# Starting the first Strassen quad of the z2 stage among the banded tiles of the last attention group

## Chip, cores, metric

One core of a Trainium2 chip. The metric is the device time of one execution in microseconds (us). Each time below is a median, with the lowest and highest run where they matter.

## The reference

```python
x = A_x                                         # 2048 tokens, 1024 wide
g = sigmoid((x * gate_w).sum(-1, keepdims=True))
# a: 32 heads of 32; each token sees 8 tokens at distances 0, 2, .. 14
logits = einsum('bhsd,bhswd->bhsw', q, kg) * Dh ** -0.5
a = einsum('bhsw,bhswd->bhsd', softmax(masked(logits)), vg) ... @ wo
# b: gMLP mixer
z  = gelu(x @ w_in)                             # 3584 wide: z1 and z2, 1792 each
gg = w_sp @ layernorm(z2) + b_sp
b  = (z1 * gg) @ w_out
return g * a + (1 - g) * b
```

## The kernel before

Matrix products run on the tensor engine (PE), the large ones as Strassen-Winograd "quads": seven products for four tiles, chained through banks of the accumulator memory (PSUM). The logits of the window attention are computed as "bands": small matmuls (L355) whose bank is evicted by ScalarE (ACT, L363), stored to memory, and loaded back in attention layout. Softmax and the products with v run elementwise on VectorE (DVE). There are eight groups of four heads. While PE multiplies for z2 and then for z1, DVE works off the rest of the attention.

One quad; `yield` separates its products:

```python
def chain(..., vs, put, share, N, flip=False, side=None, lean=False, done=None):
    def plus(out, a):
        dve(N / 960.0 + 0.14, clock["PE"] + 0.2)             # the program's own model
        last_add[0] = nc.vector.tensor_tensor(out[:, n], a[:, n], vs, ALU.add)   # L474
    if side is None:
        side = quad[0] % 2                                   # which four banks
        quad[0] += 1
    X, Y, Z, V = bank_roles[side]
    ...
    product(X, pairs(A11, B11), True, N)
    last_seed[0] = nc.scalar.copy(Y[:, n], X[:, n])          # L487, the seed
    yield
    product(V, pairs(S1, T1), True, N)
    share(vs, V[:, n])                                       # L493 on ACT; on DVE in later z1 quads
    yield
    product(Y, pairs(S2, T2), False, N)
    plus(Z, Y)
    yield
    product(X, pairs(A12, B21), False, N)
    put(0, 0, X)                                             # gelu on ACT
    yield
    product(Y, pairs(S3, T3), False, N)
    plus(V, Y)
    ...
    product(Z, pairs(S4, B22), False, N)                     # needs the first add
    ...
```

Four terms recur. The seed is the copy of X into Y (L487). The share copy, or vs copy, is the copy of V into vs (L493). The adds (L474) add vs to other banks. A mark (L559) is a short matmul that PE runs on a bank before products add onto a copied seed there.

The order of DVE's instructions is fixed when the kernel is built. The program keeps a clock for each engine. Before every add or copy it calls `advance`, which places attention operations that its model says still fit:

```python
FR, LATE, WZ_LATE = 0.4, 0.5, 4.0
def advance(t):
    while True:
        events  = [(max(i[0], clock["SP"]), 0, i) for i in due]              # DMA issues
        events += [(sub_end[g] + LATE, 1, g) for g in range(NG)              # exponentials
                   if sub_end[g] < FAR and not hold[0]]
        events += [(max(o[0], clock["DVE"]) + FR * o[1], 2 + n, o)           # DVE operations
                   for n, o in enumerate(options())]
        events = [v for v in events if v[0] <= t]
        if not events: break
        ... # emit the earliest
```

So an operation of length d is put ahead of an add that is due at t if its start plus 0.4 d is not after t. The attention products of one group half:

```python
for ws in SPLIT[g > FINE]:                # FINE = -1: always 4 operations of 2048 elements, L677
    yield ..., lambda: tt(p5[:, ws], in0[:, ws], in1[:, ws], ALU.mult)
for n, ws in enumerate([slice(0, 4)] if g <= FINE else [slice(0, 2), slice(2, 4)]):
    yield ..., lambda: tt(a, a, b, ALU.add)                    # L681, two operations
yield ...                                                      # L682, L686
```

The places that the change touches:

```python
BAND_AT = (1, 3, 6)
def among_bands(g, quad):
    for n in range(7):
        next(quad); step()
        if n + 1 in BAND_AT: band_set(g, x); ...
...
# group_tiles(7):
    return [tiles[0], band[1], tiles[1], band[0], tiles[2], band[2], tiles[3]]
...
for n in range(0, len(quads), 2):         # z2: 15 quads, two at a time
    def quad_step():
        hold[0] = count[0] != 1           # exponential held since group 7: at step 1
        if n == 0 and count[0] == 0: mark(bank_roles[1][1:3], ZC)
        step()
        count[0] += 1
    run(*[z2_quad(*q) for q in quads[n:n + 2]], step=quad_step)
```

The z1 loop:

```python
DRAIN, SUMS = 1, NFH - 2
for fp in range(NFH):
    run(z1_quad(fp, 0), z1_quad(fp, 1), ...)     # DVE makes the share copies from fp = 2 on
    if fp == DRAIN:
        drain()        # place all attention work that is left, here, as one block
```

## Time and profile before

| | before |
|---|---|
| time, median of 3 (lowest to highest) | 650.38 us (650.0 to 650.91) |
| span of the profiled run | 649.2 us |
| PE busy | 638.1 us, 98% |
| DVE busy | 519.3 us, 80% |

PE, busy for 98% of the span, sets the time here. A wait of PE is seen in the timeline as a number in brackets after its line, with the instruction that released it. What another engine costs in this kernel is read from such waits, so the reading goes from PE's waits to the engine named and then back along that engine's order. The prediction shows the lines.

### The profile page before, as it was taken

The numbers are of one execution on the slowest core, as the hardware profiler recorded it, in microseconds if no ns is written. First come the engines' busy times: TensorE is split into PE (matmuls) and PEld (weight loads), VectorE is DVE, ScalarE is ACT, GpSimd is POOL, SyncE is SP. The second block draws the span as 40 slices with busy tenths as digits, with TensorE's granted clock in tenths as the row PEclk, the third lists the DMA queues.
The fourth block names the chain that finished last, engine by engine and source line by source line (L and its number), as shares of the span: only waits on it lengthen the run. The fifth ranks groups of instructions, "written<-read, shape, count | busy, mean of one in ns | idle before, by whom it ended". The sixth has DMA issues, their size and how long they took to land.

```text
span 649.2 us, 11298 instructions
## 1 busy us (share of the span) xinstructions
PE 638.1 (98%) x4346; PEld 336.4 (52%) x4391; DVE 519.3 (80%) x816; ACT 297.8 (46%) x644; POOL 15.4 (2%) x27
## 2 busy tenths in 40 slices
PE   8999999999999999999999999999999999999997
PEld 4544467444445555444444444444444444868684
DVE  0357988999899999999988766987569999596952
ACT  3547677676776877799643121121121121212110
POOL 2210000000000000001000000000000000000000
PEclk9999999999999999999999999999999999999999
DMA  9979564798688012258994578469587383665401
GB/s 207 198 179 269 126 152 103 175 230 200 122 214 204 1 42 85 66 148 230 258 269 133 130 163 172 120 195 280 100 189 172 86 157 99 111 138 128 124 27 49
DMA packets 227174, 98.19 MB, mean 151 GB/s; under 512 B 174496, under 2 KB 214064, under 8 KB 227120
## 3 DMA queue, kind: packets, MB, share of 16 engines
q1 hardware_dynamic: 226256, 95.70, 61.2%
q0 software_dynamic: 576, 1.57, 0.9%
q8 instruction: 34, 0.56, 0.3%
q10 hardware_dynamic: 288, 0.20, 0.1%
q14 instruction: 20, 0.16, 0.1%
HBM read 44.31 MB, written 36.61 MB: 125 GB/s over the span
## 4 chain that ended last, share of the span: by engine, by line
PE 84%; ACT 4%; DVE 4%; DMA 4%; SPq 2%; issue 2%; ACTq 0%; DVEq 0%
PE psum_all L403 69%; PE psum_all L1487 8%; PE psum_all L293 4%; PE psum_all L303 2%; DMA band_d<-arena 2%; ACT arena L839 2%; PE psum_all L355 1%; DVE arena L677 1%; ACT arena L1178 1%; SPq L189 1%; DVE arena L681 1%; SPq L178 1%; DMA arena<-in_A_wqkv_dram 1%; SPq L194 1%; DVE psum_all L474 1%
## 5 line engine op out<-in xcount | busy, mean ns | idle before, releaser
L403 PE MATMUL psum_all<-arena 128*128 128x512 f16 (+6 forms) x2482 | 503.0, 362 | 3.4 <-issue 0.6
L403 PEld LDWEIGHTS <-arena 128*128 128x128 f16 (+1 forms) x2518 | 245.1, 98 | 253.8 <-issue 4.0
L677 DVE TENSOR_TENSOR arena<-arena,att_A 128x2048 f16<-128x2048 bf16 x64 | 75.5, 1219 | 0.3
L474 DVE TENSOR_TENSOR psum_all<-psum_all,arena 128x512 f32<-128x512 f32 (+1 forms) x78 | 51.0, 669 | 10.1 <-PE psum_all L403 8.3
L1487 PE MATMUL psum_all<-arena 128*128 128x256 f16 (+1 forms) x468 | 51.6, 273 | 0.0
L1487 PEld LDWEIGHTS <-arena 128*128 128x128 f16 x468 | 45.8, 98 | 5.5
L293 PE MATMUL psum_all<-arena 128*128 128x512 bf16 x183 | 42.0, 379 | 1.4 <-issue 0.8
L421 ACT COPY psum_all<-psum_all 128x512 f32<-128x512 f32 (+1 forms) x24 | 12.5, 521 | 66.8 <-PE psum_all L403 66.2
L784 ACT ACTIVATE arena<-psum_all 128x448 bf16<-128x448 f32 x64 | 34.3, 546 | 19.0 <-PE psum_all L403 9.0
L1178 ACT ACTIVATE arena<-psum_all 128x512 bf16<-128x512 f32 x56 | 31.4, 612 | 19.8 <-PE psum_all L403 9.0
L681 DVE TENSOR_TENSOR arena<-arena 128x2048 f16<-128x2048 f16 x32 | 37.9, 1218 | 0.0
L363 ACT CAST arena<-psum_all 128x1988 f16<-128x1988 f32 (+3 forms) x25 | 34.0, 1360 | 3.6 <-PE psum_all L355 3.4
L839 ACT ACTIVATE arena<-arena 128x896 bf16<-128x896 bf16 x32 | 30.9, 980 | 0.0
L546 DVE TENSOR_TENSOR arena<-arena 128x512 f16<-128x512 bf16 (+5 forms) x60 | 30.1, 534 | 0.3
L445 ACT COPY psum_all<-psum_all 128x512 f32<-128x512 f32 (+1 forms) x24 | 12.4, 519 | 37.2 <-PE psum_all L403 36.6
L293 PEld LDWEIGHTS <-arena 128*128 128x128 bf16 x192 | 18.1, 98 | 21.6 <-DMA arena<-in_A_wqkv_dram 0.7
L870 ACT CAST arena<-psum_all 128x512 bf16<-128x512 f32 x40 | 22.1, 592 | 12.5 <-DVE psum_all L474 9.6
L389 DVE TENSOR_TENSOR arena<-arena 128x2048 f16<-128x2048 bf16 x8 | 9.4, 1222 | 21.8 <-ACT gl_s L306 20.9
L427 ACT COPY arena<-psum_all 128x512 f32<-128x512 f32 (+1 forms) x24 | 12.7, 534 | 26.3 <-PE psum_all L403 22.5
L487 ACT COPY psum_all<-psum_all 128x512 f32<-128x512 f32 (+1 forms) x39 | 21.7, 570 | 6.6 <-PE psum_all L403 6.0
L432 ACT COPY psum_all<-psum_all 128x512 f32<-128x512 f32 (+1 forms) x24 | 12.5, 519 | 25.6 <-PE psum_all L403 23.0
L550 DVE TENSOR_TENSOR arena<-arena 128x1024 f16<-128x1024 f16 (+1 forms) x16 | 11.3, 714 | 15.7 <-PE psum_all L403 15.7
(113 smaller groups left out, 530.6 us busy)
## 6 DMA issues: line engine op xcount, KB each, us to landing
arena<-v_d SPq DMA_DIRECT2D x8, 960.0 KB, 7.1
z_d<-arena SPq DMA_DIRECT2D x14, 512.0 KB, 3.4
arena<-z_d SPq DMA_DIRECT2D x14, 512.0 KB, 4.1
zg_d<-arena SPq DMA_DIRECT2D x56, 128.0 KB, 2.2
arena<-zg_d SPq DMA_DIRECT2D x32, 224.0 KB, 3.2
band_d<-arena SPq DMA_DIRECT2D x28, 248.5 KB, 4.6
arena<-in_A_wqkv_dram SPq DMA_DIRECT2D x16, 256.0 KB, 4.3
o_d<-arena SPq DMA_DIRECT2D x4, 1024.0 KB, 6.3
```

Source lines behind the costliest of these rows:

```text
L293: nc.tensor.matmul(ps[:], w[:, t, kt, :], xT[:, kt, 512 * c:512 * (c + 1)], start=(kt == 0), stop=(kt == KT - 1))
L363: nc.scalar.copy(dst, src)
L403: nc.tensor.matmul(bank[:, 0:N], lhsT, rhs, start=(start and m == 0), stop=(m == n - 1), skip_group_check=True)
L474: last_add[0] = nc.vector.tensor_tensor(out[:, n], a[:, n], vs, ALU.add)
L546: return [lambda a=a: nc.vector.tensor_tensor(*a) for a in args]
L677: lambda ws=ws, in0=in0, in1=in1: tt(p5[:, ws], in0[:, ws], in1[:, ws], ALU.mult)), False
L681: lambda a=p3[:, ws], b=p3[:, ws.start + 4:ws.stop + 4]: tt(a, a, b, ALU.add)), not n
L784: nc.scalar.activation(z2[:, i + 8 * a, ZC * c:ZC * (c + 1)], bank[:, 0:ZC], ACT.Gelu_apprx_tanh, accum_out=s1[:, 4 * n + c:4 * n + c + 1])
L839: return nc.scalar.activation(junk, src, ACT.Square, accum_out=(s2, s2h)[x][:, n:n + 1])
L870: nc.scalar.copy((qT_slots, kT_slots)[t][g % 2][:, :, 256 * (c + 2 * x):256 * (c + 2 * x + 1)], bank[:].rearrange("p (n e) -> p e n", e=2))
L1178: last_gelu[0] = nc.scalar.activation(z1s[:, f, a, :], bank[:], ACT.Gelu_apprx_tanh)
L1487: nc.tensor.matmul(bank[:, h], l, r, start=(start and m == 0), stop=(m == len(ab) - 1), skip_group_check=True)
```

## The change

Intent: fill PE's wait among the last bands with the first product of the first z2 quad; evict the third band set of group 2 sooner; let the share copies of the first pair go before the exponential that is held back while group 7 is placed; and save DVE time by wider attention operations, placed while PE works on groups 5 to 7. No arithmetic is added or removed.

Counting in the traces, groups from 0: the exponential held is the seventh of eight, that of group 6. The core of the diff:

```diff
-                for ws in SPLIT[g > FINE]:
+                for ws in SPLIT[not wide[0]]:
...
-                for n, ws in enumerate([slice(0, 4)] if g <= FINE else [slice(0, 2), slice(2, 4)]):
+                for n, ws in enumerate([slice(0, 4)] if wide[0] else [slice(0, 2), slice(2, 4)]):
...
-            if n + 1 in BAND_AT:
+            if n + 1 in (BAND_AT if g != 2 else (1, 3, 5)):
...
-            tiles = [lambda a=a, m=m: z2_tile(7, a, m) for m in range(2) for a in range(2)]
+            roles = bank_roles[0]
+            tiles = [lambda n=n: z2_tile(7, n % 2, n // 2, lambda: roles[3 - n % 2]) for n in range(4)]
...
-        return [tiles[0], band[1], tiles[1], band[0], tiles[2], band[2], tiles[3]]
+        early.append(z2_quad(*quads[0], 0))
+        return [tiles[0], band[1], tiles[1], lambda: next(early[0]), band[0], tiles[2], band[2], tiles[3]]
...
         hold[0] = g == NG - 1
+        wide[0] = g in (5, 6, 7)
...
+    wide[0] = False
...
         def quad_step():
-            hold[0] = count[0] != 1
-            if n == 0 and count[0] == 0:
-                mark(bank_roles[1][1:3], ZC)
+            hold[0] = count[0] != 4
             step()
...
-        run(*[z2_quad(*q) for q in quads[n:n + 2]], step=quad_step)
+        two = [z2_quad(*q, m) for m, q in enumerate(quads[n:n + 2])]
+        if n == 0:
+            two = [two[1], early[0]]
+            next(early[0])
+            quad_step()
+            mark(bank_roles[1][1:3], ZC)
+        run(*two, step=quad_step)
```

Since each z2 quad now names its side, the shared counter that gives z1 quads their sides no longer moves by 15 in the z2 stage.

More of the change, by code (lines that the diff above doesn't have):

```diff
@@ L692, in products @@
             next_v()
+    wide = [False]
     SPLIT, FINE = [[slice(n * x, n * x + n) for x in range(8 // n)] for n in (4, 2)], FINE_TO
@@ L785, in z2_gelu, with z2_tile @@
                              accum_out=s1[:, 4 * n + c:4 * n + c + 1])
-    def z2_tile(i, a, m):
-        ps = low_bank()
+    def z2_tile(i, a, m, bank=low_bank):
+        ps = bank()
         pe(2 * T_Z)
@@ L912, in play_group @@
         return True
+    early = []
     def group_tiles(g):
```

## The prediction

> **What bounds the kernel now.** I read the head of the page first, then the longest waits of the tensor engine, then the chain of waits, then the timeline of the 20 us that the change touches.
>
> The page, parts 1 and 2:
>
> ```profile
> span 649.2 us, 11298 instructions
> PE 638.1 (98%) x4346; PEld 336.4 (52%) x4391; DVE 519.3 (80%) x816; ACT 297.8 (46%) x644; POOL 15.4 (2%) x27
> PE   8999999999999999999999999999999999999997
> PEclk9999999999999999999999999999999999999999
> ```
>
> The tensor engine (PE) is busy for 638 of 649 us at full clock. A change that removes no matmul can therefore win at most the 11 us of idle time[...]. The change removes none: it moves four matmuls of one product and leaves the marks (the two short matmuls per bank pair) as many as they were.
>
> Busy time of the engines in stretches of the timeline (columns: stretch and length, then busy us and instruction count of PE, PEld, DVE, ACT, POOL, then clock and DMA):
>
> ```profile
> 80.00:89.00 9.00, 8.40 (x105) 4.93 (x103) 8.37 (x17) 7.71 (x15) 0.00 (x0) 1.00 0.54 125
> 174.00:183.00 9.00, 8.38 (x165) 4.46 (x163) 8.72 (x15) 7.80 (x12) 0.00 (x0) 1.00 0.48 91
> 183.00:194.00 11.00, 10.59 (x56) 5.27 (x54) 10.97 (x15) 8.08 (x19) 0.00 (x0) 1.00 0.85 236
> 194.00:232.00 38.00, 38.00 (x202) 19.66 (x201) 36.84 (x51) 28.33 (x79) 0.00 (x0) 1.00 0.37 93
> ```
>
> The rest of the z2 stage (194 to 232) has no PE idle time at all. What the change can reach is the 0.6 us of each of the first two stretches and 0.4 us of the third. The fourth row also gives the price of a z2 product: 38.00 us over 202 matmuls is 0.188 us each, so 0.75 us for four. DVE, at 10.97 of 11 us, is full just where the first z2 quads run.
>
> The timeline of group 7 and the first quads (start, length, engine, line, count, idle before it and who ended it):
>
> ```profile
> 175.08 1.28 ACT L784 ACT_TABLE_LOAD   x1
> 176.91 1.81 ACT L363 CAST arena<-psum_all 128x1988 f16<-128x1988 f32 x1
> 178.77 0.27 PE L355 MATMUL psum_all<-arena 32*64 32x64 bf16 x16 [0.62 <-ACT arena L363]
> ...
> 184.01 4.62 DVE L677 TENSOR_TENSOR arena<-arena,att_A 128x2048 f16<-128x2048 bf16 x4
> 185.38 1.28 ACT L631 ACT_TABLE_LOAD   x1
> 186.67 0.63 ACT L631 ACTIVATE att_L<-att_L 128x512 f16<-128x512 f16 x1
> 187.21 0.95 ACT L493 COPY arena<-psum_all 128x448 f32<-128x448 f32 x2
> 188.88 1.16 DVE L474 TENSOR_TENSOR psum_all<-psum_all,arena 128x448 f32<-128x448 f32 x2
> 189.56 10.68 PE L403 MATMUL psum_all<-arena 128*128 128x448 f16 x54 [0.27 <-DVE psum_all L474]
> ```
>
> Two waits are seen. (1) The 16-matmul band set waits 0.62 us until ScalarE (ACT) has evicted the band set before it. (2) The fifth product of the first quad waits for the add L474. Two things hold that add: its operand, the copy L493, stands behind the exponential and its table load (until 187.7 and 188.2), and DVE itself is in four attention products until 188.63. Both end within half a microsecond of each other, so removing one alone gains little.
>
> The chain of waits says where the lateness of DVE comes from:
>
> ```profile
> 170.23 3.55 DMA band_d<-arena
> 173.82 2.09 DVE arena L546 x2
> ...
> 184.09 4.55 DVE arena L677 x4
> 188.70 0.09 issue
> 188.81 0.07 issue
> 188.88 1.16 DVE psum_all L474 x2
> 190.03 2.26 DVE arena L681 x2
> 192.29 0.56 DVE psum_all L474
> 192.89 59.22 PE psum_all L403 x312
> ```
>
> From 173.8 to 192.9 the path that sets the end runs through DVE, not ACT, and it began at a band transfer; DVE had stood 2.88 us waiting for the band loads just before 169.4.
>
> [...] the trace has 1219 ns for L677. [...] 1024 elements (L686) take 0.69 us and 2048 take 1.22, so 0.53 us per 1024 and the rest fixed. [...] The load is 1283 ns here, but the exponential starts at 186.67, 1.29 us after the load began[...]; I count 1.28. [...]
>
> **The change, part by part.**
>
> Third band set of group 2 one product earlier. Before, the mark waits for its eviction (end 85.13) with an idle gap of 0.35 us. Evicted some 0.4 us sooner, that gap closes. But at 88.03 PE waits again, for a seed copy behind a vs copy that ACT could start only at 87.23, when the second band set's store landed (87.13) and its buffer was free. That store starts at 81.45 either way. So PE arrives 0.35 us earlier at the same wall: gain about 0.
>
> First product among the bands. It puts 0.75 us of work in front of the set that waited; the start of that set was 969 ns after the matmul before it, where about 300 is usual at such a switch, so 0.66 us of wait is filled. Its seed copy (0.52 us on ACT) delays the next eviction, which then ends about 180.7, as PE arrives (180.6): minus 0.1. Gain 0.55 us. The first z2 section product now starts at 182.70 + 0.75 - 0.66 = 182.8.
>
> Exponential at step 4 instead of step 1. Both vs copies now precede the 3.2 us block of two table loads and the exponential: the adds' operands are there at 184.3 and 186.9 instead of 187.7 and 188.2. Eight gelus follow the block at about 0.52 us each (rate of a dense run), until 194.7; the next pair's third products need their seeds at about 196. No new wait on ACT.
>
> Wide operations in groups 5 to 7. Four L677 in 4.62 us become two of 1.22 + 2 x 0.53 = 2.28, with the usual 0.09 overlap 4.47 us; two L681 in 2.35 become one of 2.28. With three or four half groups touched this is 0.5 us of DVE; most of it lies before the 169.4 wait for the bands, which swallows it. About 0.13 us is left when the products of (group 5, first half) start: 183.9.
>
> The sum at the fifth product. The early quad needs its first add sooner: the fifth product follows the second by six products and two marks, 182.8 + 6 x 0.75 + 0.37 = 187.7, where the old one was ready at 182.7 + 8 x 0.75 + 0.37 = 189.1. DVE does not come sooner: by the program's own placement rule (an operation goes in front of an add if 0.4 of it fits before the add is due) both wide products are still put before the add. They end at 183.9 + 4.47 = 188.4, then 0.2 for the weights (L661) and 0.6 for the add: 189.2. So PE waits about 1.6 us there, against 0.43 before. The second wait (0.31 us at 192.9) goes, since the later adds are then far ahead of their products.
>
> Sum: -0.55 (bands) - 0.31 (second wait) + 1.2 (first wait longer) = +0.3 us. Checked by the other route: the pair ends seven products after 189.3, at 194.5; before, 192.89 + 2 x 0.75 = 194.4. Near nothing; the DVE chain sets both.
>
> **Rivals.** (a) The author's hope: the exponential was what held the adds, DVE is on time, and the waits go. For it: vs arrived at 187.7 to 188.2. Against it: DVE busy until 188.63, chain through DVE. It gives -0.66 - 0.43 - 0.31 = -1.4, and with 0.3 of the group 2 gap 648.7. (b) Coarse operations: a 2.28 us operation put before an urgent add costs up to 1.1 us more than a 1.22 us one, and delays repeat at later pairs: +1 to +2, 651.5 to 652. Against it: wide operations end with group 7, and from 194 to 260 the trace shows PE without a wait over 0.1 us, so slack exists. (c) The exponential later starves attention: its weights start only at 201.06 and 233.1, 14 us after each exponential, so 3 us do no harm: 0. (d) The z2 quads no longer take turns by the shared counter, so the first z1 quad follows the last z2 quad on the same four banks; the gelus there ended at 263.8 to 264.9 and its second product starts near 266: 0 to 0.2.
>
> **Range and chances.** My working gives 650.4 + 0.3; I give rival (a), whole or half, 40%, which pulls to 650.2. Eight in ten: 648.9 to 651.2. A gain of 2% would be 13 us, more than all idle time: 0.4%. A loss of 13 us would need a stall in every quad: 1%.
>
> **What would show it.** Right: the 16-matmul band set starts without its 0.62 us wait; the fifth product of the early quad is released by L474 with an idle time over 0.8 us while its vs copy ended before 185; the seed wait near 88 grows to about 0.6. Wrong: no wait on L474 near 188 (then rival a), or waits on L474 in later pairs (b), or on L487 at the second pair, where I see none.

The sum is -0.55 - 0.31 + 1.2 = +0.3 us, on 650.4, and with its 40% for rival (a) 650.2. The 0.53 us per 1024 elements is measured: L686 (1024 elements) takes 0.69 us, L677 (2048) 1.22, L1146 (4096) 2.29. Why a mark has to precede a product that adds onto a seed is not shown by any run; that the mark moves with the product is in the diff.

## The result

| | before | changed |
|---|---|---|
| median of six runs | 650.45 us | 650.96 us |
| lowest to highest | 650.0 to 651.83 | 650.68 to 654.17 |

A ratio here and below is from the runs of both kernels in the same rounds. It lies near the ratio of the means, and is not quite that of the medians. Here it is 1.0013, with a 95% interval of 0.9992 to 1.0034: the same, within 2%. The profiled run of the changed kernel was its longest, 654.17 us at a mean granted clock of 0.997; the other five took 650.68 to 651.48 at 1.0.

Page of the changed kernel:

```profile
span 652.4 us, 11330 instructions
PE 643.1 (99%) x4391; PEld 336.9 (52%) x4391; DVE 519.6 (80%) x807; ACT 298.4 (46%) x644; POOL 15.9 (2%) x27
PEclk9999999999989999999999999999999999999999
```

Line numbers of this kernel are shifted further down: L784 became L785, and L1174 became L1185. DVE has 9 instructions fewer, but is no less busy. PE has the same 4391 weight loads as before (45 matmul records are missing from the trace of before, so the two busy times compare only roughly; the 11 us of idle time that the prediction counts are too many for the same reason: the changed kernel, with all 4391 records, is idle for 9.3 us, though it has new waits of 2.38 and 0.91 us). New is one digit of its clock, an 8, in the slice around 190 us.

Stretches of the same run (stretch and length, then busy us and count of PE, PEld, DVE, ACT, POOL, then granted clock and DMA):

```profile
80.00:89.00 9.00, 8.71 (x107) 5.36 (x106) 8.62 (x17) 8.17 (x15) 0.00 (x0) 1.00 0.56 128
174.00:183.00 9.00, 9.00 (x168) 4.72 (x167) 8.79 (x11) 8.51 (x14) 0.00 (x0) 1.00 0.62 124
190.16:193.15 2.99, 2.99 (x10) 1.21 (x8) 2.99 (x4) 1.29 (x4) 0.00 (x0) 0.50 0.97 304
194.00:197.00 3.00, 3.00 (x18) 1.56 (x16) 2.15 (x3) 2.15 (x8) 0.00 (x0) 1.00 1.10 301
```

The first two rows are the stretches whose idle time the change was after: PE's idle time there fell from 0.60 to 0.29 and from 0.62 to 0. The third row is new: for 3 us the granted clock was 0.50, and 10 matmuls ran where 18 run in as long a stretch just after it.

Timeline of group 7 and the first quads, changed kernel:

```profile
170.36 0.29 DVE L640 TENSOR_TENSOR att_m<-att_L 128x256 f16<-128x256 f16 x1 [3.94 <-DMA att_L<-band_d]
...
178.52 0.27 PE L355 MATMUL psum_all<-arena 32*64 32x64 bf16 x16
...
183.41 0.53 ACT L493 COPY arena<-psum_all 128x448 f32<-128x448 f32 x1
184.83 4.48 DVE L677 TENSOR_TENSOR arena<-arena,att_A 128x4096 f16<-128x4096 bf16 x2
...
189.23 0.62 DVE L474 TENSOR_TENSOR psum_all<-psum_all,arena 128x448 f32<-128x448 f32 x1
189.91 25.30 PE L403 MATMUL psum_all<-arena 128*128 128x448 f16 x124 [2.38 <-DVE psum_all L474]
```

The band set at 178.52 no longer waits. The share copy is done before 184. The two wide attention operations stand ahead of the add, as predicted, but they start at 184.83, and PE waits 2.38 us instead of 0.27. The first line shows where that began: DVE waited 3.94 us for the loaded bands (2.88 before). L640 computes the maxima of a group's logits; these are the sixth of eight, so the bands are those of group 5. Where expectations below speak of the bands or the maxima of group 7, they mean this wait.

The place that the prediction never looked at is 100 us later, between the second and the third pair of z1 quads. DVE before:

```profile
285.87 3.48 DVE L677 TENSOR_TENSOR arena<-arena,att_A 128x2048 f16<-128x2048 bf16 x3
289.28 2.35 DVE L681 TENSOR_TENSOR arena<-arena 128x2048 f16<-128x2048 f16 x2
...
293.53 1.28 DVE L1174 COPY arena<-psum_all 128x512 f32<-128x512 f32 x2
```

And DVE in the changed kernel, with PE's line after it:

```profile
288.42 4.62 DVE L677 TENSOR_TENSOR arena<-arena,att_A 128x2048 f16<-128x2048 bf16 x4
292.96 2.36 DVE L681 TENSOR_TENSOR arena<-arena 128x2048 f16<-128x2048 f16 x2
...
297.21 1.28 DVE L1185 COPY arena<-psum_all 128x512 f32<-128x512 f32 x2
...
299.16 2.10 PE L403 MATMUL psum_all<-arena 128*128 128x512 f16 x9 [0.91 <-DVE psum_all L474]
```

This is the block that `drain` places ahead of the share copies of the third pair: 3 + 2 + 1 (L682) + 1 (L686) = 7 operations before, 7.74 us; 4 + 2 + 1 + 1 = 8 in the changed kernel, 8.88 us. The share copies and the adds behind them come one operation later, and PE, which had no wait there, stands idle for 0.91 us; the stage becomes 1.05 us longer.

For the experiments I cut each trace at PE's own landmarks: the marks (L559) ahead of the v quads, of group 3, of the z2 quads and of the z1 quads, the first z2 tile, and the first matmul of the last stage. Lengths in us:

| stage | before | changed, profiled run | difference |
|---|---|---|---|
| first mark to v-quad mark (holds group 2's bands) | 20.11 | 19.81 | -0.30 |
| to the mark at group 3 | 39.62 | 39.51 | -0.11 |
| to the first z2 tile | 49.48 | 49.49 | 0 |
| z2 tiles to z2 mark, without the early product (0.75) | 9.17 | 8.49 | -0.68 |
| z2 quads, with the same product (0.75) taken off before's | 79.86 | 83.42 | +3.56 |
| z1 quads and mixing by w_sp, to the last stage | 283.94 | 284.99 | +1.05 |
| sum, first mark to last stage | 486.45 | 489.98 | +3.53 |

Each sum also holds the early product (0.75) and 3.51 us between the two pairs of z1 marks, which are in no row.

The z2 row holds a wait (2.38 us) and the half-rate stretch: from 190.16 to 193.15 matmuls start 373 ns apart instead of 189, nine of them, which is 1.7 us.

### The profile page after: what moved, and what is told of

Read it like the earlier page. It is cut to its first block, busy times and chain, and to the rows that moved or that the text cites. A ratio compares the mean times of both kernels' runs of the same rounds, so it can differ in the third digit from the quotient of the medians. Undisturbed runs are those within 1.5% of the kernel's fastest.

```text
span 652.4 us, 11330 instructions
## 1 busy us (share of the span) xinstructions
PE 643.1 (99%) x4391; PEld 336.9 (52%) x4391; DVE 519.6 (80%) x807; ACT 298.4 (46%) x644; POOL 15.9 (2%) x27
## 4 chain that ended last, share of the span: by engine, by line
PE 86%; DVE 5%; ACT 4%; DMA 2%; issue 2%; SPq 1%; DVEq 0%
PE psum_all L403 70%; PE psum_all L1498 8%; PE psum_all L293 5%; PE psum_all L303 2%; ACT arena L840 2%; DVE arena L677 2%; PE psum_all L355 1%; ACT arena L1189 1%; DMA band_d<-arena 1%; DVE psum_all L474 1%; DVE arena L681 1%; SPq L178 1%; DVE arena L546 1%; DMA arena<-in_A_wqkv_dram 1%; DMA att_L<-band_d 0%
## 5 line engine op out<-in xcount | busy, mean ns | idle before, releaser
L677 DVE TENSOR_TENSOR arena<-arena,att_A 128x2048 f16<-128x2048 bf16 (+1 forms) x58 | 75.0, 1329 | 0.2
L474 DVE TENSOR_TENSOR psum_all<-psum_all,arena 128x512 f32<-128x512 f32 (+1 forms) x78 | 51.5, 671 | 13.5 <-PE psum_all L403 11.4
L785 ACT ACTIVATE arena<-psum_all 128x448 bf16<-128x448 f32 x64 | 34.3, 544 | 18.6 <-PE psum_all L403 9.6
L681 DVE TENSOR_TENSOR arena<-arena 128x2048 f16<-128x2048 f16 (+1 forms) x29 | 37.6, 1328 | 0.0
L546 DVE TENSOR_TENSOR arena<-arena 128x512 f16<-128x512 bf16 (+5 forms) x60 | 30.1, 535 | 0.4
L487 ACT COPY psum_all<-psum_all 128x512 f32<-128x512 f32 (+1 forms) x39 | 21.7, 568 | 7.3 <-PE psum_all L403 6.6
L303 PE MATMUL psum_all<-arena 128*128 128x385 bf16 x128 | 22.5, 329 | 0.5 <-DVE arena L325 0.3
```

The costliest lines, as they stand in the source:

```text
L303: nc.tensor.matmul(ps[:, 0:VP + 1], xT[:, kt, i * P:(i + 1) * P], wvp[:, kt, :], start=(kt == 0), stop=(kt == KT - 1))
L546: return [lambda a=a: nc.vector.tensor_tensor(*a) for a in args]
L677: lambda ws=ws, in0=in0, in1=in1: tt(p5[:, ws], in0[:, ws], in1[:, ws], ALU.mult)), False
L681: lambda a=p3[:, ws], b=p3[:, ws.start + 4:ws.stop + 4]: tt(a, a, b, ALU.add)), not n
L785: nc.scalar.activation(z2[:, i + 8 * a, ZC * c:ZC * (c + 1)], bank[:, 0:ZC], ACT.Gelu_apprx_tanh, accum_out=s1[:, 4 * n + c:4 * n + c + 1])
```

## The experiments

**Theory**, as it stood after all runs (the fourth term came out of experiment 4). Four terms: group 2 gains up to 0.4; the filled band wait gains 0.68; the first add loses time that depends on when the bands land; and the early start shifts DVE's placement so that one more attention product falls into the drain, +1.06. **Rivals:** the wide operations cause the losses, as coarser steps (the prediction's rival b); the later exponential causes them (its rival c); the changed sides of the banks cause them (its rival d); or the profiled run was an accident and nothing was lost.

Twelve runs were made, on three chips in three sets, all correct. "x / y" is the median of a kernel and of the kernel before in the same rounds. All differ from the kernel before by under 2%.

**1. No early product.** The changed kernel, with the first product back behind the bands:

```diff
-        return [tiles[0], band[1], tiles[1], lambda: next(early[0]), band[0], tiles[2], band[2], tiles[3]]
+        return [tiles[0], band[1], tiles[1], band[0], tiles[2], band[2], tiles[3]]
```

> The changed kernel, but the first z2 quad begins after group 7 again (the exponential stays late, the operations wide, the group 2 band early). Theory A (the early start makes the first add due about 1.4 us sooner than DVE can give it): the wait for L474 at the fifth product falls from 2.4 us to 1.0 to 1.3, the 0.62 us wait of the 16-matmul band set comes back, and the time is 0.3 to 0.7 us under the changed kernel's. Rival B (the wide operations alone make the wait): the wait stays over 2 us and the time is 0.5 us above the changed kernel's.

651.2 / 651.25, ratio 0.9996 (0.9979 to 1.0014). The band wait is back, by its old releaser:

```profile
180.11 0.27 PE L355 MATMUL psum_all<-arena 32*64 32x64 bf16 x16 [0.61 <-ACT arena L363]
```

Waits on L474 at the first pair are 0.10 and 0.15 us, less than the expected 1.0 to 1.3, the z1 stage is 283.93, and the drain has 7 operations. So the long first wait and the longer z1 stage both need the early start; wide operations and the late exponential, which this kernel keeps, make neither by themselves. First mark to last stage is 485.85, 0.60 less than before.

**2. Only the third band set of group 2.** The kernel before with

```diff
-            if n + 1 in BAND_AT:
+            if n + 1 in (BAND_AT if g != 2 else (1, 3, 5)):
```

> The kernel before with nothing but the third band set of group 2 one product earlier. The comparison of the two traces says that this part alone gains 0.40 us (the marks' wait of 0.35 us is gone and the seed wait near 88 is not longer). My prediction said 0, with a seed wait near 88 grown to 0.6 us. Expected: 0.4 us under before, PE starts the fourth row of the v quads near 87.6 in place of 88.0.

652.29 (650.47 to 656.6) / 651.25, ratio 1.0024 (0.9996 to 1.0052). The time shows no gain. The trace does: the first two stages are 19.82 and 39.51, 0.29 and 0.11 shorter than before, and the whole stretch to the last stage is 485.79, 0.66 shorter. Its runs scatter over 6 us, one at a clock of 0.997; a gain of 0.4 us cannot be read from them. Of the 0.66, 0.26 lies in z2, where the maxima came 0.26 us sooner than before. For the edit itself, all traces help: the first two stages together take 59.73 and 59.76 in the two without it (before and experiment 9), and 59.32 to 59.60 in the twelve with it. So the part gains 0.13 to 0.41, and the prediction's "about 0" was too low.

**3. Weight sums placed sooner.** The changed kernel with the sums of z2 weights (L546) released to DVE earlier in the model, so that fewer stand ahead of the first add:

```diff
-    FR, LATE, WZ_LATE = 0.4, 0.5, 4.0
+    FR, LATE, WZ_LATE = 0.4, 0.5, 1.5
```

> The changed kernel with the four sums of the z2 weights (L546, 1.05 us each) placed 2.5 us sooner in the order, into the time in which DVE stands waiting for the bands of group 7 (3.9 us in the changed kernel). Theory A (DVE is late at the first add because of that idle time): DVE idle before the maxima falls under 2 us, the add comes about 2 us sooner, the wait at the fifth product falls from 2.4 us to under 0.7, and the time is 1.5 to 2 us under the changed kernel's. Rival C (the first add is held by ACT, its copy of vs or the exponential): the wait stays over 1.5 us.

651.0 / 651.25, ratio 1.0 (0.9982 to 1.0019). The first wait fell to 0.23 us, and the z2 stage to 79.58; the z1 stage stayed at 285.00, with 8 operations in the drain and the same wait:

```profile
295.40 6.85 PE L403 MATMUL psum_all<-arena 128*128 128x512 f16 x31 [0.91 <-DVE psum_all L474]
```

So the z1 loss is a term of its own, and not a consequence of PE's long wait in z2. The times do not show the 1.5 to 2 us that were expected (651.0 beside the changed kernel's 650.96, from other rounds).

**4. DVE's model clock set forward as well.** Experiment 3 with

```diff
         hold[0] = g == NG - 1
+        if g == NG - 1:
+            clock["DVE"] += 2.0
```

so that adds go ahead of attention work in z2.

> As the run with the sums sooner, and the program's own clock for DVE is set 2.0 us later at the start of group 7, so that it puts fewer attention operations in front of the first add (two narrow ones in place of two wide ones). Theory A: no wait over 0.3 us for L474 in the first pair, and none over 0.5 us near 298; the time is 649.0 to 649.6 us, about 1 us under before. Rival C: the wait stays. Rival D (work pushed behind the add comes back as a wait in the z1 stage): the wait near 298 grows over 1.5 us.

655.9 (655.28 to 657.34) / 651.25, ratio 1.0072 (1.0053 to 1.009). This is not the gain that the edit was made for; the expectation's rival D came true. The z2 stage is the shortest of all, 78.91, with no wait at the first pair. But the attention work put off was not gone: the drain holds 11 operations, 12.12 us, and the z1 stage took 291.23:

```profile
298.43 4.00 PE L403 MATMUL psum_all<-arena 128*128 128x512 f16 x9 [4.37 <-DVE psum_all L474]
```

After these 4.37 us the clock was 0.50 for about 5 us, with matmuls 427 ns apart instead of 216; all six runs had a mean clock of 0.995 to 0.997. This was the run that showed me the drain as the place to look: 7 operations no wait, 8 a wait of 0.91, 11 a wait of 4.37. Three operations more are 3.24 us of DVE and 3.46 us of wait.

**5. The changed kernel again.** No edit.

> The changed kernel once more, for a profile in which the tensor engine keeps its full clock. Theory A: the same waits as in the first profile, 2.4 us at the fifth product of the early quad and 0.9 us near 298, and where no stretch of half-rate matmuls follows, the part from the group 1 marks to the last stage takes about 488.1 us, 1.7 us over before. If the half rate follows every such wait, it takes 490 us again.

651.68 (650.44 to 653.4) / 651.66, ratio 0.9996 (0.9974 to 1.0018). In this profiled run DVE waited 2.85 us for the bands, PE waited

```profile
189.10 7.16 PE L403 MATMUL psum_all<-arena 128*128 128x448 f16 x37 [0.94 <-DVE psum_all L474]
```

and no stretch at half rate followed. The z1 stage was 285.00 again. So the 2.38 us and the half rate belong to single executions, and the 1.06 to the kernel. First mark to last stage is 486.93; the expected 488.1 took the wait of 2.4 us for granted.

**6. Narrow operations.** The changed kernel without

```diff
-        wide[0] = g in (5, 6, 7)
```

> The changed kernel with the narrow attention operations in groups 5 to 7. Then three narrow products stand before the first add in place of two wide ones (3.5 us in place of 4.5). Theory A with the width as part of it: the wait at the fifth product falls from 2.4 us to 0.7 to 1.4; the wait near 298 stays at 0.9 us, since the attention work left for the drain is the same. Rival E (width has no part in it): it stays at 2.4 us.

651.44 / 651.66, ratio 0.9997 (0.9978 to 1.0016). The expectation was a wait of 0.7 to 1.4 us at the fifth product; the fifth product now finds its add done: the add starts 18.01 us after the maxima (L640) instead of 18.87. The wait moved to a later product:

```profile
192.79 67.74 PE L403 MATMUL psum_all<-arena 128*128 128x448 bf16 x356 [0.63 <-DVE psum_all L474]
```

The z1 stage is 284.99, the drain has 8 operations. The width moves the first add by 0.86 us; it has no part in the z1 loss.

**7. DVE's model clock set back in z2, and experiment 3.**

```diff
+        if n == 4:
+            clock["DVE"] -= 0.6
         count = [0]
```

The model then takes DVE for free 0.6 us sooner, and by the second z1 pair it has placed one attention product more ahead of the drain.

> The changed kernel with the z2 weight sums sooner (as in the third run) and the program's clock of DVE set back 0.6 us at the third pair of z2 quads, so that one or two more attention operations are placed before the drain. Theory F (each attention operation left for the drain after the second z1 quad pair is paid by PE): seven or fewer operations stand between the last add of that pair and the first DVE copy in place of eight, the wait of 0.9 us near 298 is gone, and the part from the group 1 marks to the last stage takes 485.0 to 485.2 us, 1.3 us under before. Rival G (the new taking of turns by the banks causes the wait near 298): it stays at 0.9 us.

649.29 (649.15 to 650.66) / 651.66, ratio 0.9964 (0.9946 to 0.9983): the fastest kernel, 0.36% under the kernel before, with an interval that excludes 1 (experiment 10 is the only other faster one of which that holds). The drain is back to three L677, and PE then runs from the first z1 products to the end of the mixing by w_sp without a break that the view shows, 216 ns for each matmul:

```profile
265.89 284.04 PE L403 MATMUL psum_all<-arena 128*128 128x512 f16 x1314
284.12 3.49 DVE L677 TENSOR_TENSOR arena<-arena,att_A 128x2048 f16<-128x2048 bf16 x3
```

z2 takes 79.10, z1 283.93, the whole stretch 484.59: 1.86 less than before, and less than the expected 485.0 to 485.2.

**8. Group 2 and sooner sums on the kernel before.** Experiment 2 with `WZ_LATE` 1.5.

> The kernel before with the third band set of group 2 one product earlier and the z2 weight sums sooner, nothing else: no early quad, no wide operation, exponential at its old step. Theory A (DVE's idle time before the maxima of group 7 makes the adds late): the waits of 0.43 and 0.31 us in the first pair shrink to under 0.2 in all, the 0.62 us wait of the band set stays, no wait near 292 on an add; the part from the group 1 marks to the last stage takes 485.2 to 485.6 us, about 1 us under before.

651.7 (650.25 to 654.93) / 651.66, ratio 1.0003 (0.9977 to 1.0029). A miss: the first add did not come sooner, as an L681 was placed ahead of it, and PE waited 0.51 us there, with the band wait of 0.62 in place. z1 is 283.92 with 7 operations. Sooner sums alone are not what makes experiment 7 fast.

**9. Only the early start.** The changed kernel with its three other parts undone:

```diff
-            if n + 1 in (BAND_AT if g != 2 else (1, 3, 5)):
+            if n + 1 in BAND_AT:
-        wide[0] = g in (5, 6, 7)
-            hold[0] = count[0] != 4
+            hold[0] = count[0] != 1
```

> The kernel before with the early quad alone (and the banks' turns that go with it): group 2 as before, exponential at step 1, narrow operations. Theory F (the early start puts one attention operation more behind the last add of the second z1 quad pair): eight operations are left for the drain in place of seven and PE waits 0.9 us near 295 for an add; the 0.62 us wait of the band set is gone. From the group 7 tiles to the last stage it takes 0.3 to 0.9 us more than before. Rival H (the wide operations or the late exponential leave it over): seven are left and no wait is there.

652.54 / 651.19, ratio 1.0022 (1.0 to 1.0044). The z2 stage is 79.64 and the z1 stage 285.00, with 8 operations in the drain and the same wait:

```profile
295.79 6.42 PE L403 MATMUL psum_all<-arena 128*128 128x512 f16 x28 [0.91 <-DVE psum_all L474]
```

The early start alone makes the z1 loss. The median is larger than the stages explain: first mark to last stage is 486.68, only 0.23 over before, and from the group 7 tiles on it is 0.16 over, not the expected 0.3 to 0.9. Two of its six runs took over 654.5, as single runs of the kernel before also do.

**10. The changed kernel with only the clock set back** (the edit of experiment 7 without that of 3).

> The changed kernel with the program's clock of DVE set back 0.6 us at the third pair, nothing else. Theory F: seven operations left and no wait near 295, while the wait at the fifth product of the early quad stays at 0.9 to 2.4 us as the band transfers fall. From the group 1 marks to the last stage 485.6 to 485.9 us where no half rate follows, 1 us under the changed kernel's second profile (486.93).

650.15 (649.78 to 650.76) / 651.19, ratio 0.9981 (0.9964 to 0.9998). The z1 stage is 283.93 with 7 operations, while the first z2 wait is still 0.85 us:

```profile
188.21 70.53 PE L403 MATMUL psum_all<-arena 128*128 128x448 f16 x372 [0.85 <-DVE psum_all L474]
```

The drain has three L677 again:

```profile
284.95 3.49 DVE L677 TENSOR_TENSOR arena<-arena,att_A 128x2048 f16<-128x2048 bf16 x3
```

This is the experiment that isolates the z1 term: one edit, which changes no instruction but the place of some of DVE's, takes 1.06 us out of z1. Beside experiment 5, the first two stages are 0.18 longer and z2 is 0.18 shorter.

**11. Exponential at step 1 again.** The changed kernel with

```diff
-            hold[0] = count[0] != 4
+            hold[0] = count[0] != 1
```

> The changed kernel with the exponential at its old step, between the first copies of the pair. Theory A (DVE sets the first add, not ACT): the wait at the fifth product is as in the changed kernel, 0.9 to 2.4 us by the length of DVE's idle time before the maxima, and the wait near 295 stays 0.9 us. Rival a of the prediction (the exponential held the adds): the wait grows by over 1 us beyond what the idle time explains.

652.83 (650.8 to 656.21) / 651.19, ratio 1.0026 (0.9996 to 1.0056). The first wait is 2.23 us and ends with an add that follows DVE's attention products, as in the changed kernel; the exponential's place has no part in it. z1 is 285.00. A half-rate stretch followed here too (clock 0.50 from 193.10 to 196.10), and this run took 656.21 us:

```profile
191.89 73.97 PE L403 MATMUL psum_all<-arena 128*128 128x448 f16 x380 [2.23 <-DVE psum_all L474]
```

**12. Sides as before.** The changed kernel with

```diff
         run(*two, step=quad_step)
+    quad[0] += len(quads)
```

> The changed kernel with the shared counter moved on by 15 after the z2 quads, so that the z1 quads take the banks in the old turns. Rival G (turns cause the wait near 295): it goes. Theory F: it stays at 0.9 us.

652.79 (650.95 to 654.57) / 651.19, ratio 1.002 (0.9991 to 1.0049). z1 is 285.00, with the same 0.91 us wait: the sides are not the cause. The first z2 wait was the longest of all, and the clock stayed at 1.00 after it:

```profile
190.07 72.28 PE L403 MATMUL psum_all<-arena 128*128 128x448 f16 x380 [2.59 <-DVE psum_all L474]
```

**The first add over all runs.** Five profiled runs have the same order of DVE's instructions up to the first add. Times in us, the second and third column from the start of the first z2 tile:

| run | maxima (L640) start | first add starts | add after maxima | PE's wait |
|---|---|---|---|---|
| changed, profiled | -3.60 | 15.27 | 18.87 | 2.38 |
| again (5) | -5.05 | 13.83 | 18.88 | 0.94 |
| clock set back (10) | -5.14 | 13.74 | 18.88 | 0.85 |
| exponential at step 1 (11) | -3.75 | 15.12 | 18.87 | 2.23 |
| old sides (12) | -3.40 | 15.47 | 18.87 | 2.59 |
| before | -4.88 | 14.60 | 19.48 | 0.27 |

From the maxima to the add, DVE runs a chain of fixed length, 18.87 us, with 0.41 us of gaps in all. The maxima start when the loaded bands land. So the wait is the landing plus a constant: in these five, the add minus 12.89. In the kernel before, the add minus the wait is 14.33. The change made DVE's chain 0.61 us shorter, but PE asks for the add 1.44 us sooner.

## Why the prediction was right or wrong

It gave 650.2 us with 648.9 to 651.2, and no change of 2%. That there is no such change held. The time came out higher: the median is 650.96, inside the range near its edge, while the mean of the six runs, 651.49, is outside.

The step that failed is the sum. It adds up the waits of the 20 us around the edit and takes what comes later for slack ("so slack exists"); the z1 loop is not in it. There the runs show +1.06 us: one attention product more in the drain, and PE idle for 0.91 us. That the sum of +0.3 us came near the +0.48 of the repeat's trace is luck. Of the repeat's terms listed below, those that the prediction had a number for (band wait, first and second add) come to -0.32; those that it had at 0 or did not have come to +0.82.

- **Filled band wait: right.** Predicted -0.55, measured -0.68; experiment 1 brings the wait back.
- **Group 2: mis-sized.** Predicted about 0, on the ground that PE would arrive sooner at the same wall. Measured -0.41 in the first profile (-0.30 to the v-quad mark, -0.11 in the next stage, which holds the wall). The wall is the landing of the second band set's last store, and it moved: counted from the first mark, the store landed at 22.06 and 22.09 us in the two traces without the edit, and at 21.14 to 21.94 in the eleven with it that show it. Where it landed at 21.91 or later (experiments 4, 8 and 10), the next stage took 39.74 to 39.79, elsewhere 39.51 to 39.59. So the mechanism was right, and the wall is a spread. Why the edit goes with sooner landings is not shown. The seed wait said to grow to 0.6 did not; it was under 0.2.
- **Second wait of the first pair: right.** The predicted gain of 0.31 came; the later adds were ahead of their products. No wait on L487 appeared at the second pair.
- **First add: mechanism right, size not one number.** Its releaser (L474), the wide products placed ahead of it, the copies done before 185, and DVE rather than ACT as the late engine, all held; experiment 11 confirms the last. The predicted wait of 1.6 us, counted from start to start, lies between the two that were measured in that way, 1.10 in the repeat and 2.54 in the first profile. What failed here was to take the start of DVE's chain from a single trace of before (the wait for the bands that "swallows" what lies ahead of it), as if the bands always landed there: their landing varies by 1.7 us among the five runs of one order.
- **What remains of the 1.6.** The prediction's own figures give 1.5 (189.2 less 187.7). At the landing of before (-4.88) the rule above gives a shown wait of 1.10 us, or 1.26 from start to start. The rest is for the most part the 0.2 us for L661, which stands behind the first add in the changed kernel (189.77 after 189.23). Two names in the prediction are off, without harm to its sum: the products at 183.9 are those of group 4 (32 of the 64 L677 lie ahead of them, eight per group), and the band store at 170.23, which it puts at the head of the chain, is not what DVE waited for, since DVE has only 0.45 us of gaps from the maxima at 169.40 to the add.
- **The sum: a term was missing.** The trace of before does show a wait of 0.28 us at 259.94 in the stretch that the prediction calls free of waits over 0.1; the sum does not rest on it. Rival (b) looked for repeated delays at z2 pairs; rival (c) put the cost of the later exponential at 0, and experiment 11 bears it out (z1 takes 285.00 with either place). What happened is a third thing: the modelled placement moved one L677 (1.22 us) into the z1 drain, in front of copies that PE needs, for +1.06 us. Shown by experiments 3, 5, 6, 9, 11 and 12, which all have 8 operations and 284.99 to 285.00, against 1, 2, 7, 8 and 10, which have 7 and 283.92 to 283.94. Experiment 9 ties it to the early start, 6, 11 and 12 clear the other parts, and 10 removes it alone.
- **Half rate: not foreseen.** The granted clock was 0.50 in such stretches, which followed waits of 2.38 and 2.23 us and lasted about 3.0 us; after the 4.37 us of experiment 4 it was 0.50 for about 5 us. In the first profile it cost 1.7 us (matmuls 373 ns apart instead of 189), and in experiment 11 about as much (10 matmuls in 3.00 us, where 17 ran in as long a stretch later). It is not certain to follow: a wait of 2.59 us was passed at full clock. Nor is it the change's alone: two of the 33 runs of the kernel before in the sets (654.29 and 654.55 us) have a mean clock of 0.997 too, without a trace.

With these terms the repeat (experiment 5) adds up: -0.33 (first two stages) -0.68 (band wait) -0.74 (both old waits at the first pair, 0.43 and 0.31 from start to start) +1.10 (new wait) +1.06 (drain) +0.09 (three short waits at the end of z2, 0.89 in all in place of 0.80) = +0.50; its trace is 486.93 - 486.45 = +0.48 longer. In the first profile 2.54 stands for 1.10, with 1.7 on top and group 2 at -0.41: +3.56, against +3.53 measured. The intended gain was there, and was paid back at the first add and at the drain.

The range was also too narrow for another reason. In the sets of eleven runs, the kernel before itself took 650.42 to 654.55 us; three runs had shown 0.9 us of spread. Part of that is startup: the first mark came between 64.73 and 67.25 us in these profiles, though no edit touches what lies ahead of it.

**Open.** Why the bands' landing scatters: the band store ended at 167.76 in the changed kernel's profile, after a weight load held the issuing queue for 1.60 us, but no run changed that queue alone. Whether the change makes late landings more frequent: of the traces in which DVE waited for the bands before the maxima, the maxima start later than -4 in three of eight with the early product and in none of three without it, which is too few to tell. Why the early start moves one operation into the drain: which step of the program's clocks does it was not followed. What decides whether the half rate follows a wait of 2.2 to 2.6 us. And the medians of experiments 2 and 9, which lie above what their stage lengths say, and which I take for scatter without having shown it.

## What to carry to other kernels

When an engine's order is fixed at build time by a model clock, an edit can move the placement far behind it: here a product started early, at 177.7 us, left one more L677 in the drain at 288 us, for 1.06 us. After such a change, count what stands ahead of each hard deadline, above all where leftover work is placed in one block. Before a gain on the busy engine is counted, look at the lead of the engine whose result it will ask for sooner: here PE asked for the first add 1.44 us sooner, and DVE's chain was 0.61 us shorter. If that chain starts on a transfer, take the landing from several traces: here it varied by 1.7 us among five of one order, and PE's wait with it from 0.85 to 2.59 us. Compare stages cut at landmarks of the bounding engine when the effects (here 0.4 to 1.1 us) are smaller than the scatter of whole runs (here up to 6 us): the best version here (experiment 7, -0.36%) took two edits, one that puts an attention operation back ahead of the drain (1.06 us, experiment 10) and one that places the weight sums sooner, with which z2 takes 79.10 us in place of 80.11.
